# An attention layer and a feed-forward layer in one kernel: unread products taken out of the head, query tiles 2 to 4 projected from float16 parts, batch 1's value maxima put behind w_in's splits

## The chip, the core and the metric

The kernel runs on one core of a Trainium2 chip. The metric is the device time of one execution in microseconds (us); the time of the kernel before is the median of three runs. One further execution was profiled, and all views of the profile come from it.

## What is computed

Two layers follow each other. The first is attention with random features: queries and keys (8 batches, 8 heads, 576 positions, head size 64) are projected to 128 features with `omega`, and their exponentials take the place of the softmax. The second is a feed-forward layer over all 4608 tokens, 512 to 2048 to 512, with the Mish function between its two products.

```python
def phi(x):                                   # queries and keys, both scaled
    proj = np.einsum('bhsd,md->bhsm', x, omega)
    h = proj - np.sum(x * x, axis=-1, keepdims=True) / 2.0
    h = h - np.max(h, axis=-1, keepdims=True)
    return np.exp(h) / np.sqrt(m)
q_p, k_p = phi(q_s), phi(k_s)
kv = np.einsum('bhsm,bhsd->bhmd', k_p, v)
z = np.sum(k_p, axis=2)
num = np.einsum('bhsm,bhmd->bhsd', q_p, kv)
den = np.einsum('bhsm,bhm->bhs', q_p, z)[..., None] + 1e-06
x = num / den                                 # then laid out as 4608 tokens of 512
h = x @ w_in
sp = np.where(h > 20.0, h, np.log1p(np.exp(np.minimum(h, 20.0))))
g = h * np.tanh(sp)                           # Mish
out = g @ w_out
```

## The kernel before

**Tiles.** Attention goes in query tiles of 128 tokens (`q_task`, 36 of them, t = 0 to 35) and in key units of one batch and two heads (`k_task`, four per batch). They are numbered by `nth` in the order in which they are given out: nth 0 to 3 are batch 0's keys, 4 to 7 query tiles 0 to 3, 8 to 11 batch 1's keys, 12 is query tile 4, 13 query tile 5. The feed-forward layer goes in chunks of 256 tokens, c = 0 to 3 (`ff_in`, `ff_out`, and `ff_out0` for chunk 0), and then in pairs of 512 (`pair_in`, `pair_out`).

**Number formats.** Most products take each factor as two float16 parts, a high one and a rest, and add three products. In the head that is not so: batches 0 and 1's keys, query tiles 0 to 4 (`whole` in `features`) and all of chunk 0 are multiplied in float32, so that TensorE can start before the splits are done. For a whole query tile ScalarE (ACT) takes the exponentials straight from PSUM, head by head, with the negated maximum as bias; from tile 5 on, ACT makes a high part (`in_parts`, the tile is named `sq`), GpSimd (POOL) subtracts it for the rest, and 16 float16 products give `pq`.

**The weights.** `w_in` and `w_out` arrive as 64-bit floats. `w_task` brings each of their eight blocks to float32 with a Prelu on ACT (line 198), an operation on POOL (201) and one on VectorE (DVE, 207), and takes its maximum (213). When all eight maxima of w_in are there, `scale_w` makes the scale `s_w`, and `w_split` splits block after block: the high half on ACT (line 69), the rest on DVE (line 82). The high half of block i + 1 is written over the float32 values of block i, so it waits for that block's rest. Chunk 1 and all later chunks need these splits. Batch b's values have a maximum of their own (`v_task`, line 301, four reductions per batch, then the scale `s_v`).

**Order.** `step` runs an agenda of generators slot by slot; `FIRST`, `WIS`, `WOS` and the gaps are tables of slots. The framework then puts each engine's instructions in one fixed order, by its own priorities; `behind(...)` keeps an instruction behind an earlier one of the same engine. On the chip each engine goes through its list in that order and waits where an operand is not ready. PSUM has three pools: `ps_h` (2 banks), `ps_o` (2) and `ps_a` (4), so a product also waits until an older tile has been read out of its bank. SyncE's queue (SP) issues nearly all DMAs in order, among them the transposing ones that bring a query tile's features (`qn` to `qp`) and its result (`xs` to `xT`) to the layout that TensorE needs. q, k tiles come through two buffers in turn (tag `af`), so that the load of one waits for the last reader of the last but one.

**Unread products.** `spin` (line 95) issues products that nobody reads, into a bank of `ps_o`: 13 at the start, one behind the exponentials of nth 0 and 1 each, two each behind those of query tiles 0 and 1, and two in front of the transposes of tile 0's `x`.

## Time and profile before

| | |
|---|---|
| median of three runs | 938.24 us (938.12 to 938.47) |
| the profiled execution, its own time | 937.79 us |
| its span, first to last instruction | 936.0 us |
| TensorE (PE) busy | 921.6 us, 98% |
| ScalarE (ACT) busy | 628.5 us, 67% |
| VectorE (DVE) busy | 529.6 us, 57% |
| GpSimd (POOL) busy | 231.1 us, 25% |
| HBM read / written | 46.37 MB / 9.44 MB |

The span is 1.8 us shorter than the execution's own time; the rest lies before the first and after the last instruction. Busy shares are means over the whole span: the first 150 us have all engines at work, while from about 250 us on there is mostly TensorE.

### The profile page before, as it was taken

The numbers are of one execution on the slowest core, as the hardware profiler recorded it, in microseconds if no ns is written. First come the engines' busy times: TensorE is split into PE (matmuls) and PEld (weight loads), VectorE is DVE, ScalarE is ACT, GpSimd is POOL, SyncE is SP. The second block draws the span as 40 slices with busy tenths as digits, with TensorE's granted clock in tenths as the row PEclk, the third lists the DMA queues.
The fourth block names the chain that finished last, engine by engine and source line by source line (L and its number), as shares of the span: only waits on it lengthen the run. The fifth ranks groups of instructions, "written<-read, shape, count | busy, mean of one in ns | idle before, by whom it ended". The sixth has DMA issues, their size and how long they took to land.

```text
span 936.0 us, 16681 instructions
## 1 busy us (share of the span) xinstructions
PE 921.6 (98%) x6797; PEld 532.4 (57%) x6797; DVE 529.6 (57%) x1019; ACT 628.5 (67%) x914; POOL 231.1 (25%) x143
## 2 busy tenths in 40 slices
PE   9998999999999999999999999999999999999998
PEld 6886866777655555555555555555555555444443
DVE  3899779855646784577357753784476345201200
ACT  5769998996949954897388747963887268304401
POOL 1331143541432233313232232323332121000000
PEclk9999999999999999999999999999999999999999
DMA  9975334623531256214531264203430242101001
GB/s 284 327 210 180 112 70 96 119 86 71 133 94 37 52 122 122 61 28 98 109 89 38 47 128 120 49 24 77 117 50 23 46 113 43 37 1 46 1 1 45
DMA packets 128204, 82.05 MB, mean 88 GB/s; under 512 B 106432, under 2 KB 106560, under 8 KB 128128
## 3 DMA queue, kind: packets, MB, share of 16 engines
q1 hardware_dynamic: 127392, 79.47, 34.1%
q10 hardware_dynamic: 736, 1.52, 0.6%
q8 instruction: 53, 0.87, 0.4%
q14 instruction: 23, 0.19, 0.1%
HBM read 46.37 MB, written 9.44 MB: 60 GB/s over the span
## 4 chain that ended last, share of the span: by engine, by line
PE 89%; DVE 5%; ACT 4%; issue 1%; DMA 0%; POOL 0%; ACTq 0%; DVEq 0%; POOLq 0%
PE po L745 31%; PE ph L721 31%; PE po L787 6%; PE ph L692 5%; PE pq L376 3%; PE pk L376 2%; PE pkv L490 2%; PE pn L540 2%; PE pkv L455 2%; PE po L804 1%; PE spin L97 1%; DVE wmax L213 1%; DVE w L207 1%; PE pk L391 1%; ACT ek L402 1%
## 5 line engine op out<-in xcount | busy, mean ns | idle before, releaser
L721 PE MATMUL ph<-xT,w 128*128 128x512 f16 x1344 | 298.4, 379 | 0.0
L745 PE MATMUL po<-wo,gp 128*128 128x512 f16 x1344 | 296.9, 379 | 0.0
L745 PEld LDWEIGHTS <-gp 128*128 128x128 f16 x1344 | 129.5, 98 | 149.9
L721 PEld LDWEIGHTS <-w 128*128 128x128 f16 x1344 | 129.1, 98 | 148.2
L82 DVE SCALAR_TENSOR_TENSOR gp<-h,us,gp 128x256 f16<-128x256 f32 (+6 forms) x104 | 103.7, 1013 | 121.9 <-ACT gp L69 121.6
L759 ACT ACTIVATE h<-ph,us 128x128 f32<-128x128 f32 (+6 forms) x240 | 108.0, 502 | 46.5 <-PE ph L721 42.4
L78 POOL TENSOR_TENSOR sq<-fq,sq 64x1024 f16<-64x1024 f32 x31 | 67.0, 2163 | 213.9 <-ACT sq L69 118.0
L692 PE MATMUL ph<-xT,w 128*128 128x256 f16 (+2 forms) x720 | 96.4, 290 | 1.3 <-DMA xT<-xs 0.8
L69 ACT ACTIVATE o<-po,us 128x512 f32<-128x512 f32 (+1 forms) x38 | 25.9, 682 | 98.9 <-PE po L745 92.5
L78 POOL TENSOR_TENSOR xs<-x,xs 128x512 f16<-128x512 f32 x34 | 46.0, 1353 | 157.0 <-issue 80.0
L78 POOL TENSOR_TENSOR sk<-fk,sk 64x1152 f16<-64x1152 f32 x24 | 58.3, 2431 | 90.2 <-ACT sk L69 90.1
L397 DVE TENSOR_REDUCE mxk<-pk 128x4 f32<-128x512 f32 (+1 forms) x96 | 49.9, 549 | 45.9 <-PE pk L376 33.4
L69 ACT ACTIVATE gp<-h,us 128x256 f16<-128x256 f32 (+6 forms) x104 | 73.8, 755 | 0.3
L397 DVE TENSOR_REDUCE mxq<-pq 128x4 f32<-128x512 f32 x72 | 46.6, 680 | 43.6 <-PE pq L376 39.5
L787 PE MATMUL po<-wo,g 128*128 128x512 f16 x288 | 65.4, 379 | 0.0
L78 DVE TENSOR_TENSOR qn<-eq,qn 128x1024 f16<-128x1024 f32 x31 | 39.1, 1262 | 43.0 <-ACT qn L69 43.0
L692 PEld LDWEIGHTS <-w 128*128 128x128 f16 x576 | 55.5, 98 | 10.9 <-issue 2.4
L759 ACT ACT_TABLE_LOAD x43 | 55.2, 1283 | 0.8
L69 ACT ACTIVATE sq<-fq 64x1024 f16<-64x1024 f32 x31 | 32.7, 1055 | 31.4 <-issue 29.9
L412 ACT ACT_TABLE_LOAD x39 | 50.0, 1283 | 0.7
L78 DVE TENSOR_TENSOR kp<-ek,kp 128x1152 f16<-128x1152 f32 x24 | 33.9, 1414 | 25.1 <-ACT kp L69 25.1
L78 POOL TENSOR_TENSOR vb<-vf,vb 128x640 f16<-128x640 f32 x24 | 35.9, 1499 | 46.3 <-DVE vb L71 34.5
(127 smaller groups left out, 1063.1 us busy)
## 6 DMA issues: line engine op xcount, KB each, us to landing
vf<-in_vL_dram SPq DMA_DIRECT2D x30, 325.0 KB, 3.2
out_dram<-o SPq DMA_DIRECT2D x36, 256.0 KB, 2.3
fq<-in_qT_dram SPq DMA_DIRECT2D x31, 256.0 KB, 3.4
fk<-in_kT_dram SPq DMA_DIRECT2D x24, 256.0 KB, 3.6
raw<-in_w_out_dram SPq DMA_DIRECT2D x5, 1024.0 KB, 7.1
wo<-in_w_in_dram SPq DMA_DIRECT2D x4, 1024.0 KB, 12.3
raw<-in_w_in_dram SPq DMA_DIRECT2D x4, 1024.0 KB, 14.6
wo<-in_w_out_dram SPq DMA_DIRECT2D x3, 1024.0 KB, 8.3
```

What stands on the lines that cost most here:

```text
L69: return act.activation(out, in_, AF.Copy, scale=scale)
L78: ins = eng.tensor_tensor(out=out, in0=in_, in1=hi, op=ALU.subtract)
L82: return eng.scalar_tensor_tensor(out=out, in0=in_, scalar=scale, in1=hi, op0=ALU.mult, op1=ALU.subtract)
L376: nc.tensor.matmul(out=pp[:, i, :], lhsT=left[:, o:o + P], rhs=right, start=j == 0, stop=j == len(terms) - 1,)
L397: sub = dve.tensor_reduce(out=mx[:, lo:hi], in_=pp[:, :m, :], axis=AX.X, op=ALU.max, negate=by_act)
L412: last = act.activation(e, e, AF.Exp, bias=lnt)
L455: nc.tensor.matmul(out=pkv[:, j, :], lhsT=e[:, t, :], rhs=vt[hp][:, u, :], start=i == 0, stop=i == 4,)
L692: ff_mm[0] = nc.tensor.matmul(out=ph[:, i, part], lhsT=wi(a, k, f) if c else wi0(k, f), rhs=x_two(c // 2)[:, y, k, lo:lo + CH] if c else x ...
L721: ff_mm[0] = nc.tensor.matmul(out=ph[:, 0, :], lhsT=wi(a, k, f), rhs=x[:, y, k, :], start=n == 0, stop=n == len(mm) - 1,)
L745: ff_mm[0] = nc.tensor.matmul(out=po[i], lhsT=gP[g, gr][:, a, f % FQ, i * P:(i + 1) * P], rhs=wo(y, f), start=f == 0 and (a, y) == parts[0 ...
L759: anchors["h"] = act.activation(h[:, :, lo:hi], ph[:, :, lo:hi], AF.Mish, scale=us[:, 0:1]).ins
L787: ff_mm[0] = nc.tensor.matmul(out=po[i], lhsT=gT[c, f // FG][:, a, f % FG, i * P:(i + 1) * P], rhs=wo(y, f), start=f == order[0] and (a, y ...
```

## The change

It has five parts.

1. The unread products behind the exponentials of query tiles 0 and 1, and those ahead of the transposes of tile 0's `x`, are left out; those at the start and behind nth 0 and 1 stay.
2. Query tiles 2, 3 and 4 are projected from float16 parts; the rest of their way (exponentials straight from PSUM, float32 products with the keys' sums) stays.
3. Batch 1's four value maxima are kept behind the newest rest of the weights' splits (`anchors["s"]`); before, they were kept behind the newest rest of a feed-forward tile (`"g"`), of which there was none yet.
4. Blocks 0 and 1 of w_in get their DVE operation (line 207) behind nth 5 and no longer behind nth 3.
5. The copy of the fourth key unit's sums out of PSUM goes from ACT to DVE.

Line numbers of the changed kernel differ by one or two from those before.

```diff
@@ w_task
-        with behind((AN, AO)[n][i]):
+        with behind((AD, AO)[n][i]):
             dve.scalar_tensor_tensor(
                 out=di, in0=high, scalar=3, in1=di, op0=ALU.logical_shift_left, op1=ALU.bitwise_or
             )
@@ w_split
             cast({"a": act, "d": dve}[W_HI[n][i]], dst[:, 0], src, s)
-            rest(dve, dst[:, 1], src, dst[:, 0], s)
-
+            anchors["s"] = (rest(dve, dst[:, 1], src, dst[:, 0], s).ins,)
@@ v_task
-            with behind({0: 31, 2: 30 + QF}.get(b, "g")):
+            with behind({0: 31, 1: "s", 2: 30 + QF}.get(b, "g")):
@@ features
+        by_act = whole
+        whole = whole and not (nth > 5 and (load.shape[1] == H))
         f = loaded.pop(name, None) or (fetch_pair if whole else fetch)(load, name)
...
-        by_act = whole
         e = sb.tile([P, n, M], F32, tag="ae", name=f"e{name}", bufs=2)
...
-        elif nth < 6 and nth not in (2, 3):
-            spin(2 if nth > 3 else 1, ident, e[:, 0:2, :].rearrange("p n m -> p (n m)"))
+        elif nth < 2:
+            spin(1, ident, e[:, 0:2, :].rearrange("p n m -> p (n m)"))
@@ k_task
-            cast(act, f, pkv)
+            cast(dve if nth == 3 else act, f, pkv)
@@ q_first
-        if off == 0:
-            spin(2, ident, x[:, 0:4, :].rearrange("p h d -> p (h d)"))
@@ tile_kernel
     AN = (3, 3, 4, 5, 41, 41, 41, 41)
+    AD = (5, 5) + AN[2:]
```

Since the framework orders each engine's list anew, more moves than the diff shows. Three places follow.

**ACT, query tiles 2 and 3.** The rows begin at the Prelu of w_in's last blocks (`raw`). `g_0` is chunk 0's first half, copied out of PSUM (`ph`) in four pieces; `eq` are the exponentials of tiles 2 and 3, `qp` the copies of their transposes. Before:

```order
L198 ACTIVATE raw_153<-raw_153 128x1024
L69 ACTIVATE g_0_623<-ph_0_0_0_624 128x512
L402 ACTIVATE eq_470<-pq_0_472,mxq_471 128x128 x4
L402 ACTIVATE eq_470<-pq_4_473,mxq_471 128x128 x4
L402 ACTIVATE eq_482<-pq_0_484,mxq_483 128x128 x4
L402 ACTIVATE eq_482<-pq_4_485,mxq_483 128x128 x4
L69 ACTIVATE qp_544<-pt_0_545 128x512
L69 ACTIVATE qp_544<-pt_1_551 128x512
```

With the change:

```order
L69 ACTIVATE g_0_561<-ph_0_0_0_562 128x512
L198 ACTIVATE raw_153<-raw_153 128x1024
L69 ACTIVATE sq_456<-fq_446 64x1024
L69 ACTIVATE g_0_561<-ph_0_0_2_668 128x512
L69 ACTIVATE sq_458<-fq_448 64x1024
L69 ACTIVATE g_0_561<-ph_0_1_0_690 128x512
L69 ACTIVATE g_0_561<-ph_0_1_2_702 128x512
L761 ACT_TABLE_LOAD
L761 ACTIVATE g_0_561<-g_0_561 128x2048
L402 ACT_TABLE_LOAD
L402 ACTIVATE eq_498<-pq_0_500,mxq_499 128x128 x4
L402 ACTIVATE eq_498<-pq_4_509,mxq_499 128x128 x4
```

The exponentials of tiles 2 and 3 stand behind two new casts (`sq`), behind all four pieces of `g_0` and behind its Mish (line 761), between two loads of the function table; before they stood ahead of the second piece.

**DVE, the way to w_in's scale.** `w_110` is the last block of w_in (207), `wmax` its maxima (213), `vmx` batch 1's value maxima (before on line 301), `mxq` the maxima of query tiles 2 and 3; lines 118 to 133 make the scale. Before, from the last block on:

```order
L207 SCALAR_TENSOR_TENSOR w_110<-raw_153,w_110 128x1024
L301 TENSOR_REDUCE vmx_733<-vf_0_671 128x1
L213 TENSOR_REDUCE wmax_121<-w_110 128x1
L301 TENSOR_REDUCE vmx_733<-vf_1_673 128x1
L118 TENSOR_REDUCE idle<-wmax_121 32x1 x4
L301 TENSOR_REDUCE vmx_733<-vf_2_675 128x1
L120 TENSOR_REDUCE idle<-idle 32x32
L301 TENSOR_REDUCE vmx_733<-vf_3_677 128x1
L123 STREAM_TRANSPOSE idle<-idle 32x32
L207 SCALAR_TENSOR_TENSOR wo<-wo 128x1024
L125 TENSOR_REDUCE allm_w_642<-idle 32x1 x4
L118 TENSOR_REDUCE idle<-vmx_733 32x1 x2
```

With the change, from the same operation on:

```order
L207 SCALAR_TENSOR_TENSOR w_110<-raw_153,w_110 128x1024
L397 TENSOR_REDUCE mxq_499<-pq_0_500 128x4
L397 TENSOR_REDUCE mxq_499<-pq_4_509 128x4
L397 TENSOR_REDUCE mxq_519<-pq_0_520 128x4
L397 TENSOR_REDUCE mxq_519<-pq_4_529 128x4
L213 TENSOR_REDUCE wmax_121<-w_110 128x1
L118 TENSOR_REDUCE idle<-wmax_121 32x1 x4
L120 TENSOR_REDUCE idle<-idle 32x32
L123 STREAM_TRANSPOSE idle<-idle 32x32
L125 TENSOR_REDUCE allm_w_606<-idle 32x1 x4
L141 TENSOR_SCALAR p_w_617<-allm_w_606 128x1
L130 TENSOR_SCALAR p_w_617<-p_w_617 128x1
```

The value maxima and the first operations on w_out (`wo`) no longer stand between the last block and the scale, nor does tiles 2 and 3's division (`x`, lines 596 to 605), which stood ahead of the first row and now comes behind the scale; `mxq` stands there instead.

**SP, query tile 5.** `fq` and `fk` are loads of query tiles and of batch 2's keys, `qp5` the transposing DMA of tile 5's features, `xT1` from `xs4` and `xs5` those of tiles 4 and 5's results. Before, with the numbers of the buffers kept:

```order
L336 DMA fq7_1492<-in_qT_dram 64x1024
L569 DMA_TRANSPOSE xT1_1068<-xs4_1249 128x8x128
L336 DMA fq8_1502<-in_qT_dram 64x1024
L332 DMA fk2_0_1531<-in_kT_dram 64x2x512
L332 DMA fk2_0_1531<-in_kT_dram 64x2x64
L525 DMA_TRANSPOSE qp5_1361<-qn5_1346 128x16x128
L525 DMA_TRANSPOSE qp6_1431<-qn6_1394 128x16x128
L332 DMA fk2_1_1616<-in_kT_dram 64x2x512
L332 DMA fk2_1_1616<-in_kT_dram 64x2x64
L569 DMA_TRANSPOSE xT1_1068<-xs5_1445 128x8x128
```

With the change:

```order
L335 DMA fq7_1510<-in_qT_dram 64x1024
L335 DMA fq8_1520<-in_qT_dram 64x1024
L569 DMA_TRANSPOSE xT1_1076<-xs4_1307 128x8x128
L331 DMA fk2_0_1549<-in_kT_dram 64x2x512
L525 DMA_TRANSPOSE qp5_1379<-qn5_1364 128x16x128
L331 DMA fk2_0_1549<-in_kT_dram 64x2x64
L331 DMA fk2_1_1634<-in_kT_dram 64x2x512
L331 DMA fk2_1_1634<-in_kT_dram 64x2x64
L525 DMA_TRANSPOSE qp6_1449<-qn6_1412 128x16x128
L817 DMA out_dram<-o0_0_1572 128x512
L817 DMA out_dram<-o0_1_1574 128x512
L569 DMA_TRANSPOSE xT1_1076<-xs5_1463 128x8x128
```

Between `qp5` and the transpose of `xs5` there now stand both loads of `fk2_1` and the two stores of chunk 0, and `fk2_0`, ahead of `qp5`, goes into the buffer of `fq7`. On ACT the cast of tile 7 (`sq7`), whose rest frees that buffer, stood ahead of tile 5's exponentials before and stands behind its cast `qn` now. On TensorE, 16 float16 products of `ff_out(1)` (L787 before, L785 with the change) now stand ahead of `ff_in(2)`'s first block; before, the first twelve stood behind it.

## Rows read from the trace of the kernel before

**Rows 1.** The profile's page: busy time, share of the span and instructions by engine; the clock that TensorE was granted in 40 slices of the span (9 is 90% or more of full speed); and the chain of work that ended last, by engine.

```profile
PE 921.6 (98%) x6797; PEld 532.4 (57%) x6797; DVE 529.6 (57%) x1019; ACT 628.5 (67%) x914; POOL 231.1 (25%) x143
...
PEclk9999999999999999999999999999999999999999
...
PE 89%; DVE 5%; ACT 4%; issue 1%; DMA 0%; POOL 0%; ACTq 0%; DVEq 0%; POOLq 0%
```

**Rows 2.** The longest waits of TensorE over the whole span (engine, what it was to write, line; what it waited for: us in total, times, longest).

```profile
PE po L804 <- ACT g L763: 1.8, 1, 1.8
PE pk L376 <- DVE x L556: 1.6, 1, 1.6
...
PE pq L376 <- POOL sq L78: 1.5, 1, 1.5
...
PE pk L391 <- ACT ek L402: 1.1, 1, 1.1
PE ph L692 <- DMA xT<-xs: 0.8, 1, 0.8
```

**Rows 3.** The timeline of TensorE from 25 to 46 us, and the two pieces of tile 4's projection later (start, us, engine, line, operation, out<-in, shapes, count; in brackets the idle time before it). An f32 product leaves two records, so a count of 32 is 16 products.

```profile
25.42 1.08 PE L97 MATMUL spin<-eq,ident 128*128 128x256 f32 x4
...
29.64 3.24 PE L592 MATMUL pn<-kvf,qp 128*128 128x65 f32 x28
32.72 0.39 PE L616 MATMUL px<-ident,x 128*128 128x128 f32 x2
32.94 1.03 PE L97 MATMUL spin<-x,ident 128*128 128x256 f32 x4
...
34.88 0.94 PE L692 MATMUL ph<-xT,w 128*128 128x128 f32 x6 [0.47 <-ACT xT L69]
...
41.02 2.06 PE L391 MATMUL pq<-om_f,fq 64*128 64x128 f32 x32
...
45.41 0.66 PE L581 MATMUL pt<-ident,eq 128*128 128x128 f32 x4 [1.27 <-ACT eq L402]
...
106.77 0.93 PE L391 MATMUL pq<-om_f,fq 64*128 64x128 f32 x10
...
110.36 0.71 PE L391 MATMUL pq<-om_f,fq 64*128 64x128 f32 x6
```

**Rows 4.** From the page's list of the costliest groups (busy us, mean ns of one | idle before): the two operations that make the float16 parts of a tile, and a load of ScalarE's function table; and one row of TensorE's timeline, the 16 products that project one query tile from float16 parts.

```profile
L78 POOL TENSOR_TENSOR sq<-fq,sq 64x1024 f16<-64x1024 f32 x31 | 67.0, 2163 | 213.9 <-ACT sq L69 118.0
...
L69 ACT ACTIVATE sq<-fq 64x1024 f16<-64x1024 f32 x31 | 32.7, 1055 | 31.4 <-issue 29.9
L412 ACT ACT_TABLE_LOAD x39 | 50.0, 1283 | 0.7
...
123.60 1.06 PE L376 MATMUL pq<-om,sq 128*128 128x128 f16 x16
```

**Rows 5.** The timelines of GpSimd (POOL) and VectorE (DVE) at 56 to 60 us, where both work on tensors in SBUF.

```profile
56.67 1.16 POOL L78 TENSOR_TENSOR xs<-x,xs 128x512 f16<-128x512 f32 x1 [16.15 <-ACT xs L69]
58.22 1.72 POOL L78 TENSOR_TENSOR xs<-x,xs 128x512 f16<-128x512 f32 x1 [0.38 <-ACT xs L69]
...
57.17 1.75 DVE L207 SCALAR_TENSOR_TENSOR w<-raw,w 128x1024 int32<-128x1024 int32 x1
```

**Rows 6.** The timeline of VectorE from 58 to 68 us, in the stretch that ends with w_in's scale s_w.

```profile
58.84 0.81 DVE L301 TENSOR_REDUCE vmx<-vf 128x1 f32<-128x640 f32 x1
...
66.66 1.21 DVE L213 TENSOR_REDUCE wmax<-wo 128x1 f32<-128x1024 f32 x1
...
68.04 0.13 DVE L133 TENSOR_SCALAR s_w<-s_w 128x1 f32<-128x1 f32 x1
```

**Rows 7.** The timeline of ScalarE (ACT) from 68 to 93 us: the high half of w_in's first split, the Mish over the second half of chunk 0, and the high half of the last split.

```profile
68.21 1.15 ACT L69 ACTIVATE w<-w,s_w 128x1024 f16<-128x1024 f32 x1 [1.78 <-DVE s_w L133]
...
86.88 1.91 ACT L763 ACTIVATE g<-g 128x2048 f32<-128x2048 f32 x1
...
92.17 1.13 ACT L69 ACTIVATE w<-w,s_w 128x1024 f16<-128x1024 f32 x1
```

**Rows 8.** The timeline of TensorE from 129 to 157 us: the products of ff_out0 (L804), the first `pn` of query tile 5, the first block of ff_in(2) (L692), and the first products of ff_out(1) (L787).

```profile
129.67 9.66 PE L804 MATMUL po<-wo,g 128*128 128x512 f32 x22
139.17 0.90 PE L540 MATMUL pn<-kv,qp 128*128 128x65 f16 x24
...
151.29 2.78 PE L692 MATMUL ph<-xT,w 128*128 128x256 f16 x24 [0.84 <-DMA xT<-xs]
...
154.80 2.75 PE L787 MATMUL po<-wo,g 128*128 128x512 f16 x12
```

**Rows 9.** The way of query tile 5 to the feed-forward part: the float16 rests of tiles 6 and 7 on POOL, the tile's cast to `qn` and its `x` to float16 on ACT, and the transposing DMAs of `qn` and of `x` in SyncE's queue (SPq; the time of a merged row covers waits between its pieces).

```profile
126.59 5.19 POOL L78 TENSOR_TENSOR sq<-fq,sq 64x1024 f16<-64x1024 f32 x2
...
132.03 1.05 ACT L69 ACTIVATE qn<-eq 128x1024 f16<-128x1024 f32 x1
...
145.32 0.61 ACT L69 ACTIVATE xs<-x 128x512 f16<-128x512 f32 x1
...
134.37 8.75 SPq L525 DMA_TRANSPOSE qp<-qn  x2
...
148.20 1.24 SPq L569 DMA_TRANSPOSE xT<-xs  x1
```

**Rows 10.** The first row of TensorE's timeline: the 13 unread products that stand at the start of the kernel in both versions.

```profile
1.50 4.96 PE L97 MATMUL spin<-idle 128*128 128x512 f16 x13 [1.50 <-DVE idle L92]
```

## The prediction, as put on record before the changed kernel was run

> **What bounds the kernel now.** I read the page first, to see which engine fills the span, then TensorE's waits, and then each engine's timeline where the change moves something. TensorE is busy for 98% of the span, its granted clock is full in every slice, and 89% of the chain that ended last is its own work [rows 1]. Its waits add up to little, and the last of over half a microsecond, that for `x` [rows 2], ends at 174 us; from there on TensorE runs through. So the time is TensorE's work plus its idle time in the first 175 us, and a change is worth what it takes out of either. The sum is made in these terms: the work that goes, the waits that go, the waits that come.
>
> In that stretch TensorE's list is in a fixed order and mixes work that others wait for (products of query tiles 2 to 5) with work that only has to be done (chunks 0 and 1). An idle gap appears only where an item's operand is late when its turn comes.
>
> **Work that goes.** Three sets of unread products: from 25.42 to 26.34 us, a like one at 27.2, and from 32.94 to 33.81, some 0.9 us each [rows 3], 2.7 in all. The f32 projection of tiles 2 and 3 took 2.06 us for both [rows 3]; from float16 parts a tile takes 1.06 by its row, 0.9 to the start of the next item [rows 4], so 0.2 is saved there. Tile 4's stood in two pieces, 0.87 and 0.64 us to the start of what followed [rows 3], so some 0.5 is saved there. Together the work is 3.4 us less; nothing else on TensorE is added or dropped.
>
> **Waits that go.** The waits of 1.8, 1.6, 1.5, 1.1 and 0.8 us [rows 2] and those of 1.27 and 0.47 [rows 3] lie in the stretch, together 8.6 us. I let all go and count again below what takes their place.
>
> **Waits that come, in order of time.** Times with the change are counted along the new lists, each operation at the time it took before.
>
> (a) 26 to 34 us, where the unread products were. They filled time in which tile 0 and 1's exponentials and the copies `qp` on ACT were awaited, and ACT's list there is as long as before. With them gone the 32 records of `pn` still end at 32.9, where they ended [rows 3]; then four transposes (0.5) and the copy to `xT` (0.6) bring the first product of chunk 0 to 34.0, not 34.88. So of the first 8.6 us only 6.5 are work: 2.1 us idle, of 2.7 us removed. Bounds 1.6 (the copies come earlier) and 2.7 (nothing is won).
>
> (b) 41 to 48 us, the new float16 parts. ACT gets to tile 2's cast at about 40.8, behind the last block's Prelu, and each tile costs 1.05 us on ACT and 2.16 on POOL [rows 4], one after the other: tile 2's parts are there at 44.0. TensorE is there at 42.4 (34.0, a block of 3.5 us that includes waits for tile 1, another block, and the two products ahead), so it waits 1.6 us. Tile 3 has its cast early, but POOL meets DVE: at 57 us an operation of DVE with two inputs in SBUF took 1.75 us beside POOL's 1.16, and POOL's next took 1.72 [rows 5], where each takes 1.2 alone. Such an operation (line 207) stands in DVE's list just there, so POOL's second subtraction ends at 47.3, and TensorE waits another 1.5. Together 3.1; bounds 2.0 (no meeting) and 4.2 (each pays once more).
>
> (c) About 60 us, the transposes of tiles 2 and 3. Their exponentials stand behind chunk 0's first Mish now. That ends near 57.3 (its last piece leaves TensorE at 53.5, then a copy, a table load of 1.28 [rows 4] and 1.9 for the Mish [rows 7]); a load and 16 exponentials of 0.27 follow to 62.9. TensorE arrives at 60.1 with 2.4 us of work beside it. Waits 1.0; bounds 0 and 2.5.
>
> (d) 65 to 129 us, the splits. Before, the scale was ready at 68.17 [rows 6] and the first high half began at 68.21 [rows 7]. Ahead of the scale DVE loses four value maxima at 0.73 to 0.8 each, two operations and a maximum on w_out at 1.1 [rows 6] and the division of tiles 2 and 3 (2.4): about 8 us earlier, so near 60. This gain is cut: ACT is still with the exponentials and `qp` until 65.1, so the first high half moves by 3.1 us, not 8. From there the splits alternate between ACT and DVE; by ACT's list, with its durations, the second Mish of chunk 0 ends near 84, where it ended at 88.8 [rows 7], and the last high half starts near 89.6 and not at 92.17. TensorE comes to that Mish's products at about 85, so the wait of 1.8 goes, with about 1 us of margin. The value maxima, now on DVE between 81 and 88 us, stand where the rests wait for ACT; their scale is first needed for chunk 2. Small waits for PSUM banks and for tiles 4 and 6 remain: 1.7 in all; bounds 0.5 and 3.
>
> ACT's load on this way: three casts added (3.2 us), one copy of 0.3 gone, and four table loads fewer, since exponentials and Mish alternate less. A load takes 1.283 us, and the 39 of its largest group had 0.7 us of idle time ahead of them in all [rows 4], so the four give 5.1 and ACT ends 2.3 us lighter. The Trainium skill, "ScalarE: Activation LUTs", section "What ACT_TABLE_LOAD costs", puts a drain of about 1.38 us to each load, 2.66 together: by it the four would be worth an estimated 10.6 us on ACT, and the splits would end some 5 us sooner still; the rows show no such drain here, so the sum goes by 1.283.
>
> (e) 139 to 155 us, tile 5's way into chunk 2. Before: its cast `qn` at 132.0, the rest on DVE, the transpose issued at 134.37, `pn` at 139.17, `x` to float16 on ACT at 145.3, its rest on POOL, the last transpose at 148.2, and chunk 2's first block at 151.29 after a wait of 0.8 [rows 8, 9]. In the new list `qn` comes at about 134, since tile 4's and 6's casts stand ahead. Its transpose then stands in SP's queue behind a load into tile 7's buffer, which waits for tile 7's rest on POOL; before, that rest was done at 131.8 [rows 9], ahead of the transpose. Now its cast follows `qn` on ACT, so 1.05 and 2.16 us [rows 4] put the transpose near 138. From issue to block the way took 16.9 us; shorter by what stood between, 15 to 17, it ends at 153 to 155. TensorE has cover: 16 products of chunk 1's output stand ahead of the block now, 3.45 us at 2.6 per twelve [rows 8], so it gets there at about 153. I take 1.5 us of waiting, tile 5's and 6's own `pn` included; bounds 0 and 4.
>
> (f) 174 us, the wait of 1.6 for tile 7's `x` [rows 2]. ACT reaches that tile's exponentials some 2 us sooner: I take 1.0; bounds 0 and 1.6.
>
> **Sum.** Waits that come: 2.1 + 3.1 + 1.0 + 1.7 + 1.5 + 1.0 = 10.4, against 8.6 that go, so 1.8 us more idle. With 3.4 less work the span falls by 1.6 us, from 936.0 to 934.4. The profiled execution took 937.79, 1.8 more than its span and 0.45 less than the median of 938.24; so its successor would take 936.2 and the median **936.6 us**. All lower bounds give 4.1 of waits and 930.3; all upper ones 18.0 and 944.2. They don't fall together; about 3.5 us to either side holds most of it: **933.2 to 940.2**. A measurement of this kernel tells 0.2%, 1.9 us, from no change: faster is below 936.4, slower above 940.1.
>
> **Rivals.**
>
> *The lead is kept.* If ACT and POOL are an operation or two ahead of my count, (d) and (e) are near their lower bounds, chunk 2's block is on time at 151, and 3 us more are won: 932 to 934.5. For it: four table loads fewer on an engine that was busy all through 83 to 125 us. Against: the meeting of POOL and DVE, which the count of ACT does not see.
>
> *The cover eats it.* TensorE's order is good but the unread products were idle time anyway and (b) costs its upper bound: 937.5 to 939.5, no change. For it: 2.1 of the 2.7 us stay as gaps.
>
> *Slower, by SP's queue.* Tile 5's transpose behind the load for batch 2 is the one place where a late operation holds four others in a row (DVE, ACT, POOL, a DMA). The block would be level with before, 3.45 us of work pulled ahead, at 154.7; beyond 157.7 the kernel is slower by more than 0.2%. That needs `qp5` issued 3 us later than I count, near 141: one further wait of tile 7's cast on ACT for its load would do. At 159 the time is about 941.5.
>
> *The clock falls.* The granted clock reads full in all slices of before [rows 1]; but the 13 products at the start take 0.38 us each [rows 10] where 512 columns take 0.22 later [rows 8], so a slow stretch cost 2.1 us there. If the gaps of (a) and (b) bring a granted clock of half, 1.2 GHz, in 30 to 48 us, one or two such stretches come on top: 939 to 941. The Trainium skill, "TensorE: Matmul & The Clock Gate", section "What's actually happening", says that half rate is the default and activity lifts it; by it, products that nobody reads can pay. Against: gaps of 1.8 us before left the clock full [rows 1, 2].
>
> **Chances.** My forecast, 935 to 937.5: 0.38; the lead kept: 0.24; the cover eats it: 0.21; SP's queue: 0.12; the clock: 0.05. My forecast lies on the faster side of 936.4 for about six tenths, so faster 0.47, same 0.37, slower 0.16 (half the clock's cases and SP's, with the ends of the others).
>
> **What would show it.** (a) chunk 0's first block near 34.0 and TensorE less than 80% busy in 26 to 34 us; (b) two waits of `pq` for POOL of about 1.5 us; (c) a wait of `pt` for ACT near 61; (d) the scale near 60, the first high half near 65, no wait of `po` for the Mish; (e) `qp5` issued near 138 and chunk 2's first block at 153 to 155 with 16 products of L785 ahead; (f) a shorter wait at 174. The forecast is wrong if `s_w` stays near 68, or if the block of chunk 2 comes before 151 or after 157.

## The result, and the profile after

The changed kernel is slower: 946.74 us (median of 5, 945.14 to 948.86) against 938.24, a ratio of 1.0095 with a 95% interval of 1.0084 to 1.0106. The forecast was 936.6 us, and 946.74 lies above its range. The profiled execution took 945.14 us with a span of 943.4, 7.4 more than before, and it was the fastest of the five: its mean granted clock was 0.998, that of the other four 0.992 to 0.994, while the profiled execution of before had 1.000.

The page of the changed kernel: busy time by engine, the granted clock in 40 slices, and the chain by engine.

```profile
PE 923.2 (98%) x6785; PEld 529.9 (56%) x6785; DVE 539.5 (57%) x1020; ACT 626.4 (66%) x912; POOL 237.5 (25%) x146
...
PEclk9999999999999999999999999999999999999999
...
PE 86%; DVE 5%; ACT 3%; DMA 3%; issue 1%; POOL 1%; SPq 0%; ACTq 0%; POOLq 0%; DVEq 0%
```

Against [rows 1] TensorE is busy for 1.6 us more, where 3.4 less was expected, and DMA has 3% of the chain. So 5.8 us of the 7.4 are new idle time. Its longest waits:

```profile
PE pq L376 <- POOL sq L78: 3.8, 3, 1.8
PE pn L540 <- DMA qp<-qn: 3.0, 2, 1.8
PE pt L581 <- ACT eq L402: 2.3, 4, 1.2
PE pk L376 <- DVE x L556: 2.2, 1, 2.2
...
PE ph L690 <- DMA xT<-xs: 0.9, 1, 0.9
PE po L785 <- ACT o L69: 0.7, 1, 0.7
```

The wait of `po` for the Mish is gone [rows 2], as forecast. The one wait of 1.5 us for GpSimd's subtraction has become three of 3.8 together, and two for tile 5's and 6's transposes (`qp`) have come. TensorE's timeline where tile 5 comes in (columns as in [rows 3]):

```profile
146.68 0.92 PE L540 MATMUL pn<-kv,qp 128*128 128x65 f16 x24 [1.80 <-DMA qp<-qn]
...
151.81 2.53 PE L785 MATMUL po<-wo,g 128*128 128x512 f16 x11 [0.71 <-ACT o L69]
155.57 0.92 PE L540 MATMUL pn<-kv,qp 128*128 128x65 f16 x24 [1.22 <-DMA qp<-qn]
...
159.41 2.78 PE L690 MATMUL ph<-xT,w 128*128 128x256 f16 x24 [0.95 <-DMA xT<-xs]
...
180.36 0.62 PE L376 MATMUL pk<-om,sk 128*128 128x128 f16 x8 [2.20 <-DVE x L556]
180.81 4.44 PE L785 MATMUL po<-wo,g 128*128 128x512 f16 x12
```

Chunk 2's first block starts at 159.41, 8.1 us later than before [rows 8], 3.45 of them for products that stand ahead of it now. After the gap ahead of 180.36 twelve products take 4.44 us where 2.6 is their usual time [rows 8]: there, from 181 to 185 us, the granted clock was half. Why tile 5 is late stands on four other engines. VectorE's subtraction for tile 5's `qn` in the kernel before:

```profile
133.11 1.23 DVE L78 TENSOR_TENSOR qn<-eq,qn 128x1024 f16<-128x1024 f32 x1 [0.93 <-ACT qn L69]
```

ScalarE, VectorE, GpSimd and SP's queue in the execution of the changed kernel:

```profile
136.05 1.04 ACT L69 ACTIVATE qn<-eq 128x1024 f16<-128x1024 f32 x1
136.99 1.04 ACT L69 ACTIVATE sq<-fq 64x1024 f16<-64x1024 f32 x1
...
137.51 1.27 DVE L82 SCALAR_TENSOR_TENSOR wo<-wo,s_w 128x1024 f16<-128x1024 f32 x1
138.70 3.15 DVE L78 TENSOR_TENSOR qn<-eq,qn 128x1024 f16<-128x1024 f32 x1
141.77 3.14 DVE L82 SCALAR_TENSOR_TENSOR wo<-wo,s_w 128x1024 f16<-128x1024 f32 x1
...
138.16 2.60 POOL L78 TENSOR_TENSOR sq<-fq,sq 64x1024 f16<-64x1024 f32 x1 [5.25 <-ACT sq L69]
141.13 2.70 POOL L78 TENSOR_TENSOR sq<-fq,sq 64x1024 f16<-64x1024 f32 x1 [0.36 <-ACT sq L69]
...
140.79 0.59 SPq L331 DMA_DIRECT2D fk<-in_kT_dram  x1
141.88 2.71 SPq L525 DMA_TRANSPOSE qp<-qn  x1
```

Tile 5's cast `qn` comes at 136.05, not 132.03 [rows 9]. Tile 7's cast follows it, so that tile's subtraction starts on GpSimd at 138.16, half a microsecond ahead of VectorE's subtraction for `qn`. That one took 1.23 us before and takes 3.15: it ends at 141.85, 1.1 us after GpSimd is done. The next pair repeats it (3.14 beside 2.70). The transpose `qp5` is issued at 141.88, 7.5 us later than before [rows 9] and 4 later than forecast. The Trainium skill, "SBUF — State Buffer", section "SBUF: two separate sides", describes an exclusive lock: of a VectorE operation with two inputs in SBUF and a GpSimd operation that reads SBUF, the one that starts first keeps the port pair for its whole duration. These rows agree with that, GpSimd's own time too: its 2.60 us, against 2.12 without a meeting, begin while VectorE's operation of 137.51 is still running.

### The profile page after: what moved, and what is told of

Its sections match the earlier page's. It is cut to its first block, busy times and chain, and to the rows that moved or that the text cites. A ratio compares the mean times of both kernels' runs of the same rounds, so it can differ in the third digit from the quotient of the medians.

```text
span 943.4 us, 16661 instructions
## 1 busy us (share of the span) xinstructions
PE 923.2 (98%) x6785; PEld 529.9 (56%) x6785; DVE 539.5 (57%) x1020; ACT 626.4 (66%) x912; POOL 237.5 (25%) x146
## 4 chain that ended last, share of the span: by engine, by line
PE 86%; DVE 5%; ACT 3%; DMA 3%; issue 1%; POOL 1%; SPq 0%; ACTq 0%; POOLq 0%; DVEq 0%
PE po L743 31%; PE ph L719 31%; PE po L785 6%; PE ph L690 5%; PE pq L376 3%; PE pkv L490 2%; PE pk L376 2%; PE pn L540 2%; DMA fq<-in_qT_dram 1%; PE pkv L455 1%; PE pk L391 1%; DMA qp<-qn 1%; DVE wo L82 1%; ACT eq L402 1%; PE spin L97 1%
## 5 line engine op out<-in xcount | busy, mean ns | idle before, releaser
L78 POOL TENSOR_TENSOR sq<-fq,sq 64x1024 f16<-64x1024 f32 x34 | 74.6, 2196 | 210.2 <-ACT sq L69 134.4
L785 PE MATMUL po<-wo,g 128*128 128x512 f16 x288 | 67.3, 386 | 0.7 <-ACT o L69 0.7
L78 DVE TENSOR_TENSOR qn<-eq,qn 128x1024 f16<-128x1024 f32 x31 | 41.1, 1325 | 42.3 <-ACT qn L69 42.2
L69 ACT ACTIVATE sq<-fq 64x1024 f16<-64x1024 f32 x34 | 35.9, 1055 | 31.6 <-issue 29.7
L69 ACT ACTIVATE xs<-x 128x512 f16<-128x512 f32 x34 | 21.3, 626 | 39.8 <-DVE x L556 30.7
```

The costliest lines, as they stand in the source:

```text
L69: return act.activation(out, in_, AF.Copy, scale=scale)
L78: ins = eng.tensor_tensor(out=out, in0=in_, in1=hi, op=ALU.subtract)
L785: ff_mm[0] = nc.tensor.matmul(out=po[i], lhsT=gT[c, f // FG][:, a, f % FG, i * P:(i + 1) * P], rhs=wo(y, f), start=f == order[0] and (a, y ...
```

## The experiments

Runs sent to one chip together share their runs of the kernel before (938.4 to 938.7 us). "Subtraction" always means the rest of a query tile's split (`in_parts`), by default on GpSimd. Behind a time stand the lowest and highest of its executions, behind a ratio its 95% interval; a clock is the mean granted clock of an execution, as a share of full speed. In the profile a window's columns are: stretch, length, busy us (and instructions) of PE, PEld, DVE, ACT, POOL, then PEclk, DMA share and GB/s.

**e1: tile 4 in float32 again.**

```diff
-        whole = whole and not (nth > 5 and (load.shape[1] == H))
+        whole = whole and not (nth in (6, 7) and (load.shape[1] == H))
```

> The changed kernel with tile 4 alone projected in float32 again; tiles 2 and 3 keep their float16 parts. Its lists then have tile 7's cast ahead of tile 5's qn on ScalarE, and both loads of fk2_0 ahead of qp5 in SP's queue, as the kernel before has them, while the scale of w_in stays early. Theory A (tile 5's way): tile 4's parts are what made it late, so qp5 is issued near 134 to 137 us, chunk 2's first block starts near 150 to 153 and not at 159.4, the granted clock is 0.998 or more, and the time is 934 to 939 us. Theory B (the parts of tiles 2 and 3, or the unread products that are missing): the time stays at 943 to 949 us.

945.21 us (942.86 to 945.36), ratio 1.0066 (1.0054 to 1.0078), clock 0.993 to 0.996. The lists are as intended, and tile 5's block starts at 154.1, 5.3 us sooner and a little behind theory A's 150 to 153, yet the time hardly falls. Theory A in its first form, that tile 4's parts are what costs, falls.

**e2: tiles 2 to 4 in float32 again; the other parts stay.**

```diff
-        whole = whole and not (nth > 5 and (load.shape[1] == H))
+        whole = whole
```

> The changed kernel with tiles 2, 3 and 4 all projected in float32 again; the unread products stay out and the value maxima stay behind the splits. Theory A: tile 5's way is as before, the granted clock full, the time 935 to 940 us. Theory B in the form of the missing unread products: the gaps of 26 to 34 us stay, so the clock still falls and the time is 943 to 949 us.

940.01 us (939.4 to 942.93), ratio 1.0027 (1.0015 to 1.0038). Of the 8.5 us lost, 6.7 are gone: the float16 parts are the main cause. The executions with a clock of 0.998 or more took 939.4 to 940.4 us, those with 0.991 and 0.993 942.9 and 942.1.

**e3: the unread products back, the parts stay.**

```diff
-        elif nth < 2:
-            spin(1, ident, ...)
+        elif nth < 6 and nth not in (2, 3):
+            spin(2 if nth > 3 else 1, ident, ...)
...
+        if off == 0:
+            spin(2, ident, x[:, 0:4, :].rearrange("p h d -> p (h d)"))
```

> The changed kernel with the unread products of tiles 0 and 1 put back (six, as before). Theory A: nothing on tile 5's way changes, so the time is 945 to 949 us, at most 1 us more than the changed kernel, with a granted clock of 0.991 to 0.998. Theory B (unread products held the clock or filled only idle time): 938 to 942 us.

945.22 us (944.73 to 946.77), ratio 1.0076 (1.0064 to 1.0088), clock 0.997 to 1.000. The products cost nothing that can be told: TensorE issues about 3 us more, and the median is 1.5 us lower than without, though the ranges overlap (945.14 to 948.86 without). What returns is the clock, which theory A had not expected. All waits of tile 5's way are there as in the changed kernel, 1.7 us later, in a profile with the clock full; so those waits are no result of the clock.

**e4: tile 4 alone from float16 parts.** The condition of e1's line is `nth > 7`.

> The changed kernel with tiles 2 and 3 in float32 again and tile 4 from float16 parts. Here qp5 stands ahead of fk2_0 in SP's queue, but tile 7's cast still follows qn5 on ScalarE and its subtraction on GpSimd can fall beside VectorE's qn5. Theory A by the meeting of the two engines: VectorE's qn5 takes about 3 us again, chunk 2's first block starts after 156, 942 to 948 us. Theory A by SP's queue alone: qp5 near 138 to 139, 937 to 940 us. Theory B (tiles 2 and 3): 936 to 939 us.

942.3 us (941.77 to 945.49), ratio 1.0051 (1.0038 to 1.0064). The median lies in the range of the meeting, but the meeting isn't there: VectorE's `qn` takes 1.21 us at 141.64, and GpSimd starts at 142.78. Chunk 2's first block still starts at 158.61, so that sign alone doesn't show a meeting. What is there is a slow head, in the profiled execution of 945.25 us:

```profile
30.00:40.00 10.00, 9.80 (x49) 9.20 (x49) 5.98 (x16) 3.83 (x6) 3.77 (x4) 0.52 1.01 314
```

Nothing of the kind is in [rows 1]. The execution with a clock of 1.000 took 941.77, e2's took 939.4. So tile 4's parts alone cost some 2.4 us, and the clock some 3.5 more when it falls (945.25 and 945.49 at 0.992 and 0.993; the profiled one is at half clock from 81 to 85 us as well).

**e5: as e3, with the subtractions of tiles 7 and 8 on VectorE.**

```diff
-        rest(by("lo", nth), ks[D:P], f, ks[0:D])
+        rest(dve if nth in (15, 16) else by("lo", nth), ks[D:P], f, ks[0:D])
```

> The changed kernel with its unread products back (as in the run before with them), and the subtractions of tiles 7 and 8 on VectorE instead of GpSimd, so nothing runs on GpSimd beside tile 5's qn5. Compared with the run with the products back (945.2 us, qn5's rest 3.14 us from 140.42, qp5 issued at 143.59, chunk 2's first block at 161.1). Theory A1 (the meeting of GpSimd and VectorE delays tile 5): qn5's rest takes 1.2 us, qp5 is issued near 141.7, the block starts near 159 and the time is 1.5 to 2.5 us less, 942.5 to 944. Theory A2 (tile 5 is late on ScalarE already, and the two subtractions only change which engine is late): within 0.8 us of 945.2.

942.41 us (941.59 to 942.77), ratio 1.0038 (1.0025 to 1.0052), clock 0.999 to 1.000: 2.8 us less than e3. VectorE, SP's queue and TensorE:

```profile
140.42 1.21 DVE L78 TENSOR_TENSOR qn<-eq,qn 128x1024 f16<-128x1024 f32 x1
...
141.66 1.98 SPq L525 DMA_TRANSPOSE qp<-qn  x1
...
156.69 2.78 PE L692 MATMUL ph<-xT,w 128*128 128x256 f16 x24 [0.66 <-DMA xT<-xs]
```

`qn` starts when it did in e3, takes 1.21 us and not 3.14, `qp5` leaves 1.9 us earlier, as expected, and the block comes at 156.69 and not 161.12. Some 2 us of these 4.4 are order and no gain: 7 products of chunk 1 stand ahead of the block here, 16 in e3. Theory A1 holds for this stretch, with a gain slightly over its range.

**e6: as e3, with batch 2's first loads on GpSimd's queue.**

```diff
-                nc.sync.dma_start(
+                (nc.gpsimd if name in ("k2_0", "k2_1") else nc.sync).dma_start(
```

> The changed kernel with its unread products back, and the loads of batch 2's first two key units issued from GpSimd's queue instead of SP's, behind the subtractions that free their buffers. SP then has nothing between tile 4's transpose and qp5. Theory SP's queue: qp5 is issued 1.5 to 3 us earlier than 143.59, time 942 to 943.5. Theory A1 (qn5's rest on VectorE ends at 143.56 whatever SP does): qp5 stays at 143.6, time 944.4 to 946.

947.57 us (946.08 to 948.67), ratio 1.0095 (1.0081 to 1.0109), clock 0.995 to 0.997. With SP's queue empty ahead of it, `qp5` is issued at 143.36, 0.2 us earlier than in e3, right behind VectorE's `qn`. The queue was not what held it; VectorE was.

```profile
140.19 3.15 DVE L78 TENSOR_TENSOR qn<-eq,qn 128x1024 f16<-128x1024 f32 x1
143.26 3.92 DVE L82 SCALAR_TENSOR_TENSOR wo<-wo,s_w 128x1024 f16<-128x1024 f32 x1
...
143.36 3.04 SPq L525 DMA_TRANSPOSE qp<-qn  x1
```

The time is above the 944.4 to 946 expected for A1, and why is not shown. VectorE's next operation takes 3.92 us, where GpSimd now issues loads behind its subtraction; but in the profiled execution TensorE idles 0.6 us less than in e3's and is busy for 1.5 more, with half clock from 181 to 185 us.

**e7: the kernel before with the float16 parts alone.** The three lines with `by_act` and `whole` of the change, nothing else.

> The kernel before with one part of the change alone: tiles 2 to 4 projected from float16 parts; unread products, value maxima and copies as before. In this list both pieces of fk2_0 and the first of fk2_1 stand ahead of qp5 in SP's queue, and tile 7's cast ahead of qn5 on ScalarE. If the parts are what costs, the time is 943 to 948 us with a granted clock of 0.997 or more; with fk2_1, whose buffer frees behind tile 8's subtraction, ahead of qp5 it should be at least that of the run with the products back, 945.2. If it is another part of the change, 937 to 940.

948.63 us (947.88 to 949.61), ratio 1.0108 (1.0094 to 1.0122). The parts alone do as much harm as the whole change (the intervals overlap), and some 3 us more than e3, which has the three small parts beside them. The expected clock of 0.997 was wrong: it was 0.992 to 0.995, although all unread products are there. TensorE's waits show where the gap was:

```profile
PE pq L376 <- POOL sq L78: 4.2, 1, 4.2
PE pn L540 <- DMA qp<-qn: 3.0, 1, 3.0
```

The 4.2 us lie ahead of tile 2's projection, and the granted clock is half from 45 to 53 us, from within that wait on. Two more such stretches follow, from 151 and from 165 us.

**e8: the three small parts alone** (value maxima behind `"s"`, two operations on w_in behind nth 5, one copy on VectorE).

> The kernel before with the three small parts of the change alone: value maxima behind the splits, two operations on w_in later, one copy on VectorE. If the parts in float16 and the missing products are the whole of it, this is the kernel before within 0.15%: 937 to 940 us, clock 0.997 or more. If moving the value maxima is worth something by itself, the scale comes earlier and the time is 934 to 937.

939.51 us (938.0 to 940.68), ratio 1.0008 (0.9999 to 1.0016): no change that can be told. The scale isn't earlier either: `s_w` is ready at 70.2 us, before at 68.2.

**e9: the changed kernel with the subtractions of tiles 7 and 8 on VectorE** (e5 without the six unread products; the edit is e5's).

> The changed kernel with one difference: the subtractions of tiles 7 and 8 on VectorE. It is the run e5 without the six unread products. e5 took 942.4 us with a granted clock of 1.000 in all executions. Theory C1 (the clock falls behind the gaps of tile 5's way, 140 to 182 us, which are shorter here): clock 0.998 or more, 941 to 943 us. Theory C2 (it falls behind the gaps of the head, where the unread products were): slow stretches in 26 to 50 us, clock 0.992 to 0.997, 943.5 to 946 us.

944.09 us (943.89 to 944.17), ratio 1.0059 (1.0045 to 1.0072), clock 0.994 to 0.996 in all five. This is C2: 1.7 us more than with the products, and the slow stretch lies in the head.

```profile
20.00:30.00 10.00, 8.80 (x86) 7.89 (x86) 5.46 (x8) 9.71 (x29) 4.62 (x3) 0.97 1.05 387
30.00:40.00 10.00, 9.80 (x49) 9.20 (x48) 6.05 (x15) 3.57 (x5) 3.34 (x3) 0.52 1.06 319
```

TensorE is busy for 8.80 of the ten us in which the products are missing, and the clock is half from 29 to 39 us.

**e10: a version meant to win**, tile 4 in float32 (e1's line), products back (e3's), subtractions of tiles 2, 3, 7 and 8 on VectorE (`nth in (6, 7, 15, 16)`).

> A version meant to win: unread products as before, tiles 2 and 3 from float16 parts with their subtractions on VectorE, tile 4 in float32, the subtractions of tiles 7 and 8 on VectorE. If GpSimd's subtractions, 2.16 us each and beside VectorE, are what the parts of tiles 2 and 3 cost, the wait of pq at 42 to 48 us falls from 2.6 us to under 1 and the time is 935 to 938. If it is the casts on ScalarE and the exponentials behind chunk 0's first Mish, it stays at 939 to 943.

937.37 us (936.7 to 938.56), ratio 0.9988 (0.9979 to 0.9997): within the range expected if GpSimd is what costs, and 7.8 us below e1, which lacks the products as well as the four moves. No `pq` waits at 42 to 48 us.

**e11: the kernel before with the subtractions of tiles 7 and 8 on VectorE.**

> The kernel before with one difference: the subtractions of tiles 7 and 8 on VectorE. There tile 5's qn5 does not meet them (1.23 us at 133.1), so theory A1 gives no change, 938 to 940 us. If work of GpSimd beside VectorE costs wherever it stands, it gains 1 to 2 us: 936 to 937.5.

942.21 us (940.54 to 942.73), ratio 1.0035 (1.0022 to 1.0047): slower, which neither theory expected. On VectorE tile 7's subtraction now stands ahead of tile 5's `qn`, and the waits of TensorE at 170 to 178 us grew:

```profile
171.43 2.78 PE L692 MATMUL ph<-xT,w 128*128 128x256 f16 x24 [1.17 <-ACT h L759]
...
177.73 1.01 PE L376 MATMUL pk<-om,sk 128*128 128x128 f16 x8 [2.21 <-DVE x L556]
```

Before, the second was 1.6 [rows 2] and the first wasn't there. A place on VectorE has its price as well. The first wait goes back in part to the same meeting at another place, VectorE's operation on w_out behind the subtraction of a key unit on GpSimd:

```profile
155.01 3.24 DVE L82 SCALAR_TENSOR_TENSOR wo<-w,s_w,wo 128x1024 f16<-128x1024 f32 x1
...
154.81 2.37 POOL L78 TENSOR_TENSOR sk<-fk,sk 64x1152 f16<-64x1152 f32 x1
```

Before, VectorE's took 1.26 us, at 157.49. The next `qn` on VectorE now comes at 164.19 and not 160.96, its transpose at 165.48 and not 162.25; ScalarE waits 2.7 us for that transpose, and the copy `h` for which TensorE waits comes behind. How much of the 3.8 us this accounts for no run shows; the profiled execution also has half clock from 178 to 182 us.

**e12: as e5, with the subtractions of tiles 2 and 3 on VectorE too** (`nth in (6, 7, 15, 16)`).

> The run e5 (942.4 us) with the subtractions of tiles 2 and 3 on VectorE as well; tile 4 still from float16 parts. If the wait of 3.1 us for the parts at 42 to 48 us is lost for good, 940 to 941 us. If TensorE only waits elsewhere for what it gained there (tiles 2 and 3's exponentials, tile 5), 941.8 to 943.

935.85 us (935.77 to 936.56), ratio **0.9973** (0.9963 to 0.9983), clock 0.999 to 1.000: faster than both kernels, and 6.6 us below e5 where at most 2.4 were expected. TensorE and VectorE at the place of the old gap:

```profile
45.20 1.07 PE L376 MATMUL pq<-om,sq 128*128 128x128 f16 x16
46.10 0.65 PE L692 MATMUL ph<-xT,w 128*128 128x256 f32 x2
46.67 1.07 PE L376 MATMUL pq<-om,sq 128*128 128x128 f16 x16
...
43.92 1.22 DVE L78 TENSOR_TENSOR sq<-fq,sq 64x1024 f16<-64x1024 f32 x1
...
45.40 1.22 DVE L78 TENSOR_TENSOR sq<-fq,sq 64x1024 f16<-64x1024 f32 x1
```

A subtraction takes 1.22 us here; on GpSimd it took 2.1 alone and up to 2.7 in the meetings above. Neither projection waits, the transposes of tiles 2 and 3 don't wait for their exponentials either, `qp5` goes out at 137.68, and chunk 2's block starts at 152.69.

**e13: as e3, with the subtractions of tiles 2 and 3 alone on VectorE.**

> The changed kernel with its unread products back and only the subtractions of tiles 2 and 3 moved from GpSimd to VectorE (those of tiles 7 and 8 stay on GpSimd). Between the run with the products back (945.2), e5 (tiles 7 and 8 alone moved: 942.4) and e12 (all four moved: 935.85). If the head's wait for GpSimd is the larger part, 936.5 to 939; if tile 5's way keeps its own price of 2.8 us, near 938.6; if the two pay only together, 941 to 943.

938.95 us (938.31 to 939.74), ratio 1.0004 (0.9996 to 1.0013): 6.3 us below e3. So the head is the larger part, and tile 5's way adds 3.1 (e12 against e13). TensorE's idle time, summed over windows of ten us, puts it in place: up to 70 us e3 has 6.0 us and e13 2.7; from 130 to 190 us 8.1 and 5.1. So half of the gain comes out on tile 5's way, whose cast `qn` starts on ScalarE at 133.89 and not at 137.77 as in e3. Whether GpSimd costs by its meeting with VectorE or by its longer operation is not separated: in the head of the changed kernel its two subtractions take 5.19 us [below, (b)], where two alone take 4.2 and two on VectorE 2.4. The order also moved the meeting: VectorE's `qn` stands at 136.53 with 1.21 us, ahead of GpSimd's pair.

```profile
136.53 1.21 DVE L78 TENSOR_TENSOR qn<-eq,qn 128x1024 f16<-128x1024 f32 x1
138.62 2.27 DVE L82 SCALAR_TENSOR_TENSOR wo<-wo,s_w 128x1024 f16<-128x1024 f32 x1 [0.87 <-ACT wo L69]
...
137.68 5.20 POOL L78 TENSOR_TENSOR sq<-fq,sq 64x1024 f16<-64x1024 f32 x2 [6.93 <-ACT sq L69]
```

**e14: the changed kernel with those four subtractions on VectorE** (e12 without the six unread products).

> The changed kernel with one difference: the subtractions of tiles 2, 3, 7 and 8 on VectorE. It is e12 (935.85 us) without the six unread products. If the clock falls behind the gaps of 26 to 34 us, which stay, the mean granted clock is 0.993 to 0.997 with a slow stretch that begins near 29 us, and the time is 937 to 940. If the products only filled idle time, 934.5 to 936.5.

941.53 us (937.69 to 941.94), ratio 1.0023 (1.0014 to 1.0033). The median is above the expected 940, since the twelve executions fall into two groups: three with a clock of 1.000 took 937.69, 938.33 and 939.0 us, nine with 0.995 took 941.42 to 941.94. The profile is of the second kind.

```profile
30.00:40.00 10.00, 9.80 (x50) 9.20 (x50) 6.11 (x16) 3.73 (x6) 3.29 (x3) 0.54 1.04 308
```

The same program, then, pays some 3.2 us (941.53 against the middle of the three) when the head's clock falls. With the products (e12) the clock was 0.999 or 1.000 in all eight.

**e15: the changed kernel, a second profile.**

> The changed kernel itself once more, for a second profile: its first one had a granted clock of 0.998 and one slow stretch, at 181 us, where its other executions had 0.992 to 0.994. If the missing unread products are what lowers the clock there, a profile with such a clock shows a slow stretch in 26 to 50 us of some 10 us beside the one at 181. If not, there are more stretches behind 140 us and none before.

948.48 us, clock 0.992, with the two slow stretches that were expected:

```profile
30.00:40.00 10.00, 9.80 (x49) 9.20 (x49) 5.98 (x15) 3.83 (x6) 3.34 (x3) 0.52 1.05 316
...
180.00:190.00 10.00, 7.80 (x88) 5.01 (x87) 8.96 (x22) 9.91 (x12) 6.77 (x4) 0.83 0.58 134
```

The first profile has 1.00 in 30 to 40 us. So its other executions, by their clock, are like this one, and this is the usual case.

## Why the prediction was wrong, step by step

The step that failed is (e), tile 5's way: 1.5 us of waiting were counted, and 4.7 came. The cast `qn` was 2 us later than counted, since what the head loses in (b) reaches it, and VectorE's subtraction for it met GpSimd's, 1.9 us more. Half clock, a rival with a chance of 0.05, came on top.

**Work that goes** was right as work: the unread products are 3.1 us of records, the projections 0.5 less. It was not right as time: no pair of runs with and without the products is faster without (below).

**(a)** Right in its time. Chunk 0's first block came at 34.57, in an execution whose 13 start products took 0.7 us more than in [rows 10]; without that, 33.9 against 34.0. The other sign missed: TensorE was busy for 84% of 26 to 34 us, forecast at less than 80. Its gaps there are 1.20 and 0.23 us, and another 0.5 us lie in the records of the transposes `pt` (3.24 us against 2.75).

**(b)** Right in size and cause, wrong in what hangs on it. The waits were 1.80 and 1.08 us against 1.6 and 1.5, and the meeting is there:

```profile
44.85 1.07 PE L376 MATMUL pq<-om,sq 128*128 128x128 f16 x16 [1.80 <-POOL sq L78]
...
47.92 1.07 PE L376 MATMUL pq<-om,sq 128*128 128x128 f16 x16 [1.08 <-POOL sq L78]
...
42.67 5.19 POOL L78 TENSOR_TENSOR sq<-fq,sq 64x1024 f16<-64x1024 f32 x2 [1.34 <-DMA fq<-in_qT_dram]
...
43.69 2.19 DVE L207 SCALAR_TENSOR_TENSOR w<-raw,w 128x1024 int32<-128x1024 int32 x1
```

The text took the 3.1 us as a term of its own. e13 against e3 shows that with the two subtractions off GpSimd the end is 6.3 us earlier, 3.3 of them by less idle time up to 70 us and the rest behind 130.

**(c)** Two waits of 0.37 us at 62.6 and 63.7, 0.7 against 1.0. But transposes that follow exponentials head by head also hide waiting in their own records: the 40 records of `pt` are busy for 8.0 us and were 6.4.

**(d)** Right at its start. `s_w` was ready at 61.2, the first high half began at 65.29, and `po` doesn't wait for the Mish. But the lead was lost on the way: the Mish ended at 85.81 (counted: 84), and the last high half began at 91.32 (89.6), 0.85 us sooner than before. Nor do the value maxima bring the scale forward by themselves: it is ready at 70.2 in e8 and 69.0 in e2, where they are moved and tiles 2 and 3 stay in float32, and at 63.9 in e7, where only the float16 parts are there. The small waits between 70 and 140 us sum to 2.3, counted at 1.7.

**(e)** Here it failed. Counted: `qn` at 134, `qp5` near 138, block at 153 to 155, 1.5 us of waiting. Measured: 136.05, 141.88, 159.41, and waits of 1.80, 0.71, 1.22 and 0.95, together 4.7. The prediction named the place, SP's queue, and its rival even gave the time of `qp5` (141). But it charged the wait to the load ahead in that queue; e6 took that load away and `qp5` moved by 0.2 us. Of the 3.9 us by which `qp5` was late, 2 are ScalarE's cast `qn`; e13 against e3, where it comes 3.9 us sooner without GpSimd's two subtractions in the head, shows that the head's delay reaches it. The other 1.9 are VectorE's `qn`, behind GpSimd's subtraction of tile 7 (e5). That meeting had been seen and priced in (b), from [rows 5], and was not asked for in (e), though the lists put tile 7's cast right behind `qn`.

**(f)** 2.2 us against 1.0, not shorter but longer. VectorE's two casts of values (L71, 1.73 us) ahead of that `x` start 1.1 us behind the first product of its `pn`, before 0.5.

**The sum.** In the profiled execution TensorE is idle for 5.8 us more than before and not 1.8: (e) has 3.2 more than counted, (f) 1.2 and (d) 0.6, while (a) to (c) have some 1.1 less. TensorE's busy time is 5.0 us over the count: 1.9 in the slow stretch at 181 (288 products of `po`, 67.3 us against 65.4), 1.6 in `pt`, 0.7 in the start products, the rest in small pieces. 4.0 and 5.0 make the 8.9 us between 936.2 and 945.14, within rounding. That execution had no slow head; the median, 946.74, is of the four with a lower clock.

**The rival of the clock** was given 0.05 and, alone, 939 to 941. The mechanism and the place (30 to 48 us) were right: e9, e14 and e15 show half clock, 1.2 GHz, from about 29 to 40 us when the products are missing. For the changed kernel it is, by the clocks, the usual case and not a rare one, and it came on top of the rest. The argument against it, that gaps of 1.8 us had left the clock full, doesn't hold by size: in e15 half clock begins at 30.3 us behind one gap of 1.2, while in the first profile the clock stayed full behind the same gap and behind the one of 1.80 ahead of 44.85. The products were worth 1.7 us between e5 and e9 and 5.7 between e12 and e14, of which 3.2 are the clock; the 1.5 between e3 and the changed kernel, and the 0.5 between e8 and e2 with the tiles in float32, are within their scatter. The Trainium skill, "TensorE: Matmul & The Clock Gate", section "What's actually happening", says that half rate is the default and that activity lifts it. The two clear pairs agree with that.

**SP's queue** gave about 941.5 us for a block at 159. The profiled execution had it at 159.41 and took 945.14: behind the block lie the slow stretch at 181 (1.9) and the longer wait of (f), 1.2 over the count.

**The lead kept** failed for the reason given against it. **The cover eats it** named half of the truth: no pair gains by leaving the products out, not even e14 at full clock against e12.

What stays open: why e14's executions at full clock (937.7 to 939.0) are still some 2 us above e12 (its profile, at the lower clock, has waits that e12 lacks: 1.8 us of `po` for the Mish, 1.7 of `pt`), how e11's 3.8 us are made up, and what makes the head's clock fall in one execution and not in another.

## What to carry to other kernels

An operation on GpSimd is to be charged at every place where the new order puts it beside a two-input operation of VectorE, not only where it is added. A wait is to be followed on: what it delays on the engines behind it can cost as much again as the wait itself. Where a mostly idle engine is late with a short operation that TensorE waits for, the busier engine that does it in half the time can be better: moving four subtractions turned a loss of 0.76% (e3) into a gain of 0.27% (e12). It isn't so everywhere: in the kernel before, two such moves cost 0.35% (e11). Products that nobody reads are not simply idle time to be saved: from 20 to 40 us the clock was full in all ten profiles that have them there, and in three of the seven without.

## What the runs showed of the hardware

VectorE's two-input subtraction of 128 x 1024 took 1.21 us alone and 3.14 or 3.15 when a GpSimd subtraction had started 0.5 us ahead of it; it ended 1.1 us after GpSimd did. GpSimd's own, 2.12 alone, took 2.6 to 2.7 there, begun while VectorE's operation before was still running.

The granted clock of one program differs between executions: in e14 nine of twelve had a mean of 0.995 and three 1.000, 3.2 us apart. From 26 to 30 us TensorE was busy for 2.8 of the four us in all seven profiles without the six products. In four of them (e4, e9, e14, e15) half clock began at 29 to 30 us and lasted some ten; in the changed kernel's first profile, e1 and e2 the clock stayed full up to 40 us, as in all ten profiles with the products. e3, e5 and e12, with the products, never showed a mean below 0.997; e6 and e7, with them too, did (0.995 and 0.992), and their profiles have the half clock later, from 181 and from 45 us on.
